# Layer 1 of a two-layer MoE behind banded and strided attention: token blocks of 512, 256 and four of 384 instead of six of 384

## The chip, the cores and the metric

The kernel runs on one core of a Trainium2 chip. The metric is the device time of one execution in microseconds. The engines are TensorE (PE; its weight loads are listed as PEld), VectorE (DVE), ScalarE (ACT), GpSimd (POOL) and SyncE (SP), which issues all DMAs here.

## The reference

Attention over 4 batches, 8 heads, 576 positions of 64 dimensions; the first four heads see the last 32 positions, the other four every 32nd position back. Its output, 2304 tokens of 512, goes through two dense layers of 2048 hidden units:

```python
scores = np.matmul(q, k.transpose(0, 1, 3, 2)) / np.sqrt(D)
mask_local = (rel >= 0) & (rel < 32)                       # heads 0 to 3
mask_strided = (rel >= 0) & (pos[None, :] % 32 == pos[:, None] % 32)   # heads 4 to 7
attn = softmax(np.where(mask, scores, -1e9)) ; x = (attn @ v) as (2304, 512)
h = np.maximum(x @ w_in, 0.0) ; x = (h * h) @ w_out        # layer 1
h = x @ w_in2 ; P = a0 + a1*h + a2*h*h + a3*h**3 ; Q = 1 + |b0|*|h| + |b1|*h*h
out = (P / (Q + 1e-6)) @ w_out2                            # layer 2
```

The weights arrive as 64-bit floats.

## The kernel before

The tokens are cut into six blocks of 384 (`TB`). A layer goes block by block; in a block the 16 hidden tiles `f` of 128 units are its steps. A step has a hidden unit (`h_unit`, L383: 12 matmuls of 128x128 by 384 columns, four slices `kk` of x times three products of high and low halves) and, two steps later (`LAG`), an output unit (`o_unit1`, L423: 12 more), which adds into four PSUM banks `acc`. Between them `act1` makes relu, square, a high part `gh` (ScalarE) and a low part `gl` (DVE in block 0, GpSimd later). At a block's end `evac1` stores the sums into a scratch in DRAM, from which layer 2 loads its x again (`load_x1`). Layer 2 works on 384-token blocks in the same way with a rational function (`act2`), its output units (L608) with 512 columns and six units behind.

Weights come as pairs of 32-bit words. `to_f32` (L161 on ScalarE, L162 to L164 on DVE) makes float32 of half a tile of weights and `split_w` (L180, L181 on GpSimd) its high and low parts. In block 0 `feed_w(2)` converts two halves each step, up to eight raw loads ahead; raw tiles lie in places of weight tiles not yet in use (`homes`). In blocks 1 to 4 the weights of layer 2 are converted in the same way and spilled to DRAM (`spills` counts halves by block).

Attention is cut into 14 pieces (`ORDER`): for each batch two strided ones (heads 4 and 5, 6 and 7), for each token block a local one (heads 0 to 3). Pieces 0 to 2 run first, ahead of all else, since block 0 needs them: strided, strided, local. The others are put between the steps of layer 1 by `PLAN`: at step (j, f) the scores and the softmax and the load of the next piece's queries and keys, two steps later the transposes of the exponentials, a step after that the values and x (`at_out`: a high copy on ScalarE, the low rest on DVE). x has three pairs of tiles in turn, each with all four slices: slices 0 and 1 are the local heads, 2 and 3 the strided ones.

A scheduler orders each engine's instructions when the kernel is built, by program order among what it takes to be ready, and places waits; instructions in `keep` stay in program order on their engine. SP's queue is in order too: a load that waits for its buffer holds those behind it.

The last five steps of layer 1's last block (`EARLY`) alternate with the first five units of layer 2, and among those `unit2` issues loads of layer 2's next block:

```python
if j + 1 < NB and f in (1, 4, 7, 10):
    load_x1(j + 1, f // 3)
```

Of the kernel before, what the change touches and what calls it, by code (L numbers as in the profile page):

```python
# [25 lines left out]
NB = NT // TB  # L26
# [38 lines left out]
def _local_window(J, j):  # L65

    first = (TB * J + STRIDE * j) % S == 0
    return STRIDE * j + (STRIDE if first else 0)


def _pack_qkv(q, k, v):

    tok = lambda x: x.transpose(1, 0, 2, 3).reshape(H, NT, D)
    qs = np.zeros((B * 2, P, QKS_W), np.float32)
    vs = np.zeros((B * 2, P, 2, 6, D), np.float32)
    a, c3 = np.arange(NA), np.arange(3)
# [13 lines left out]
    vl = np.zeros((NB, 2, P, 12, D), np.float32)  # L90
    qt, kt, vt = tok(q), tok(k), tok(v)
    for J in range(NB):
        for hp in range(2):
            for r in range(2):
                h, rows, t0 = 2 * hp + r, slice(r * D, (r + 1) * D), TB * J
                ql[J, hp, rows, :TB] = qt[h, t0 : t0 + TB].T
                lo = max(0, t0 - STRIDE)
                ql[J, hp, rows, TB + STRIDE - (t0 - lo) :] = kt[h, lo : t0 + TB].T
                for j in range(12):
                    w0 = t0 - STRIDE + _local_window(J, j)  # L100
                    vl[J, r, hp * D : (hp + 1) * D, j] = vt[h, w0 : w0 + 64]
    return qs, vs.reshape(B * 2, P, V_W), ql, vl.reshape(NB, 2, P, V_W)
# [8 lines left out]
def moe_kernel(ctx, tc, qs, vs, ql, vl, w1, w2, a, b, masks, eye, out):  # L111
    nc = tc.nc

    x1_dram = nc.dram_tensor("x1_scratch", (NB, P, KT * TB), F32, kind="Internal").ap()
# [5 lines left out]
    xpool = ctx.enter_context(tc.tile_pool(name="xpool", bufs=6))  # L120
# [9 lines left out]
    sms = [cpool.tile([P, 24], F32, name=f"sm{i}") for i in range(4)]  # L130
# [88 lines left out]
    def load_qk(p):  # L219
        if p.strided:  # L220
# [3 lines left out]
            return  # L224
        for hp in range(2):
            if p.n < HEAD:
                t = wpool.tile([P, QKL_W], F32, tag=("wh7", "wl7")[hp], name=f"qk{p.name}_{hp}")
            else:
                t = apool.tile([P, QKL_W], F32, tag="qk", name=f"qk{p.name}_{hp}")
            nc.sync.dma_start(t, ql[p.at, hp])  # L230
            p.qk.append(t)

    def load_v(p):
# [5 lines left out]
        for r in range(2):  # L239
            if p.n < HEAD:  # L240
                t = wpool.tile([P, 12, D], F32, tag=("wh6", "wl6")[r], name=f"v{p.name}_{r}")
            else:
                t = apool.tile([P, 12, D], F32, tag="v", name=f"v{p.name}_{r}")
            nc.sync.dma_start(t, vl[p.at, r].rearrange("p (j d) -> p j d", d=D))
            p.v.append(t)

    def at_scores(p):
# [5 lines left out]
        for r in range(2):  # L253
            flat = p.ps[r][:, : 6 * p.w]
# [28 lines left out]
        for m in range(3):  # L283
            for hp in range(2):
                for c in range(4):
                    j = 4 * m + c
                    k0 = QL_W + _local_window(p.at, j)
# [4 lines left out]
    def at_softmax(p, r):  # L292
        sm = sms[(2 * p.n + r) % len(sms)]
        to, mask = p.masks[r]
        s3 = p.ps[r][:, : 6 * p.w].rearrange("p (a k) -> p a k", k=p.w)
        if p.n >= MASK_PE:
            nc.vector.tensor_tensor(to, to, mask, ALU.add)
        nc.vector.tensor_reduce(sm[:, 0:6], s3, AX.X, ALU.max)  # L298
# [8 lines left out]
        wide = lambda c: sm[:, c : c + 6, None].to_broadcast([P, 6, p.w])  # L307
        nc.vector.tensor_tensor(ev, s3, wide(0), ALU.subtract)
        nc.scalar.activation(ev, ev, AF.Exp, scale=1.0 / 8.0)
        nc.vector.tensor_reduce(sm[:, 6:12], ev, AX.X, ALU.add)  # L310
        nc.vector.tensor_scalar(sm[:, 12:18], sm[:, 6:12], 1e-9, None, ALU.add)
        nc.vector.reciprocal(sm[:, 18:24], sm[:, 12:18])
        nc.gpsimd.tensor_tensor(ev, ev, wide(18), ALU.mult)
# [12 lines left out]
    def at_values(p):
# [15 lines left out]
        for j in range(12):  # L342
# [9 lines left out]
    def at_out(p):  # L352
        if not p.strided:
            x = x_block(p.at)
            for hp in range(2):
                split_x([z[:, hp, :] for z in x], p.o[hp][:, :TB])
            return
        a0 = 0
        while a0 < NA:
            t0 = p.at * S + a0 * STRIDE  # L360
            na = min(NA - a0, (TB - t0 % TB) // STRIDE)
            x = x_block(t0 // TB)
            for i, (base, nu) in enumerate(S_SLOTS):
                views = [
                    z[:, p.hp, t0 % TB : t0 % TB + na * STRIDE]
# [19 lines left out]
    def act1(j, f, ps):  # L385
        psum_h = j == NB - 1 and f >= NF - EARLY
        if psum_h:
            nc.scalar.activation(ps[:, :TB], ps[:, :TB], AF.Relu)
            nc.scalar.activation(ps[:, :TB], ps[:, :TB], AF.Square)
            h = ps[:, :TB]  # L390
        else:
            h = gpool.tile([P, TB], F32, tag="r", name=f"r{j}_{f}", bufs=4)
            nc.scalar.activation(h, ps[:, :TB], AF.Relu)  # L393
# [4 lines left out]
        gh = gpool.tile([P, TB], F32R, tag="gh", name=f"gh0_{j}_{f}", bufs=3)  # L398
        gl = gpool.tile([P, TB], F32R, tag="gl", name=f"gl0_{j}_{f}", bufs=3)
# [15 lines left out]
    def o_unit1(j, f):  # L415
# [4 lines left out]
        for e in range(KT):  # L420
            c = slice(DM + e * P, DM + (e + 1) * P)
            for i, (w, g) in enumerate(((wh, gh), (wh, gl), (wl, gh))):
                nc.tensor.matmul(acc[j][e][:, :TB], w[:, c], g, start=(f == 0 and i == 0), stop=(f == NF - 1 and i == 2))  # L423

    def evac1(j):
        for e, p in enumerate(acc.pop(j)):
            t = gpool.tile([P, TB], F32, tag="r", name=f"x1_{j}_{e}", bufs=4)
            if e % 2:
                nc.vector.tensor_copy(t, p[:, :TB])
            else:  # L430
                nc.scalar.copy(t, p[:, :TB])
            nc.sync.dma_start(x1_dram[j][:, e * TB : (e + 1) * TB], t)
# [3 lines left out]
    warm = gpool.tile([P, TB], F32, tag="r", name="warm", bufs=4).bitcast(BF16)[:, :512]  # L436
# [121 lines left out]
    def act2(j, f, ps):  # L558
# [74 lines left out]
    PLAN = {3: (0, 0), 4: (0, 5), 5: (0, 10), 6: (1, 1), 7: (1, 7), 8: (2, 0), 9: (2, 5), 10: (2, 10), 11: (3, 0), 12: (3, 5), 13: (3, 10)}  # L633
# [22 lines left out]
    spills = (0, 8, 16, 24, 2 * NF)  # L656
# [57 lines left out]
```

## Time and profile before

| | us |
|---|---|
| median of 3 runs | 893.65 (893.38 to 894.51) |
| the profiled execution | 892.89 |
| its span on the core | 891.1 |
| PE busy | 865.2 (97%) |
| DVE busy | 624.5 (70%) |
| GpSimd busy | 535.0 (60%) |
| ScalarE busy | 486.4 (55%) |

The span is the time between the first and the last instruction on the core. Busy times are unions of an engine's instructions. Matmuls overlap in the records, so their lengths say less than the distances between their starts.

### The profile page before, as it was taken

What the parts mean: (1) busy time and instruction counts of PE and PEld (TensorE: products, weight loads), DVE (VectorE), ACT (ScalarE), POOL (GpSimd) and SP (SyncE); (2) the same over time, 40 slices, a digit from 0 to 9 for tenths busy, and PEclk for the clock granted to TensorE, in tenths of its full rate; (3) what the DMA queues carried; (4) which work ended last, traced back from release to release, by engine and by line L of the source; (5) the groups of instructions that cost most, each with busy time, mean ns of one, the idle gap of its engine ahead of it and who ended that gap; (6) DMA issues with size and microseconds to landing.
All of it is one profiled execution on the core that took longest, in us unless ns stands there. A gap on an engine that the chain in (4) does not pass through costs nothing.

```text
span 891.1 us, 16392 instructions
## 1 busy us (share of the span) xinstructions
PE 865.2 (97%) x6312; PEld 807.2 (91%) x6312; DVE 624.5 (70%) x791; ACT 486.4 (55%) x1017; POOL 535.0 (60%) x555
## 2 busy tenths in 40 slices
PE   6798899999999999999999999999999999999998
PEld 4688789999999999999999999999999999999996
DVE  6798884655656765344115798888888888888885
ACT  4455533433433433333236777767767867867763
POOL 2477664444544544543234687877877877776773
PEclk8799999999999999999999999999999999999999
DMA  9881455645455443532684500100100100000000
GB/s 346 298 306 55 138 169 180 192 151 167 143 202 167 142 133 97 176 119 74 228 295 171 187 18 10 50 13 10 50 14 10 47 17 10 35 1 1 36 1 35
DMA packets 38957, 100.10 MB, mean 112 GB/s; under 512 B 4576, under 2 KB 10976, under 8 KB 38880
## 3 DMA queue, kind: packets, MB, share of 16 engines
q1 hardware_dynamic: 38880, 99.07, 32.5%
q8 instruction: 49, 0.80, 0.4%
q14 instruction: 28, 0.23, 0.1%
HBM read 72.84 MB, written 26.21 MB: 111 GB/s over the span
## 4 chain that ended last, share of the span: by engine, by line
PE 86%; DVE 5%; DMA 3%; ACT 2%; POOL 2%; issue 1%; SPq 0%; POOLq 0%; DVEq 0%; ACTq 0%
PE h L383 42%; PE acc L608 22%; PE acc L423 18%; PE ps_vl L330 1%; DMA qks<-in_qs 1%; DMA qkl<-in_ql 1%; PE ps_vs L330 1%; PE ps_tl L320 1%; DVE r L397 1%; POOL wl L181 1%; PE ps_sl L269 1%; DVE sm L298 1%; ACT w L161 1%; DVE w L164 1%; DVE sm L310 1%
## 5 line engine op out<-in xcount | busy, mean ns | idle before, releaser
L383 PE MATMUL h<-xh,wh 128*128 128x384 f32 x768 | 262.4, 342 | 1.0 <-POOL wh L180 0.4
L383 PE MATMUL h<-xh,wl 128*128 128x384 f32 x768 | 259.4, 338 | 1.3 <-POOL wl L181 1.2
L383 PE MATMUL h<-xl,wh 128*128 128x384 f32 x768 | 258.8, 337 | 0.0
L577 DVE RECIPROCAL h<-w 128x384 f32<-128x384 f32 x96 | 245.2, 2554 | 0.7 <-POOL w L574 0.7
L573 POOL TENSOR_TENSOR p<-p,hs 128x384 f32<-128x384 f32 x96 | 97.6, 1017 | 112.8 <-ACT p L571 112.8
L383 PEld LDWEIGHTS h<-xh,wh 128*128 128x128 f32 x768 | 145.3, 189 | 7.5 <-POOL wh L180 1.2
L383 PEld LDWEIGHTS h<-xl,wh 128*128 128x128 f32 x768 | 145.1, 189 | 4.1 <-DVE xl L350 0.2
L383 PEld LDWEIGHTS h<-xh,wl 128*128 128x128 f32 x768 | 145.1, 189 | 2.5 <-POOL wl L181 2.4
L401 POOL TENSOR_TENSOR gl<-r,gh 128x384 fp32r<-128x384 f32 x75 | 76.8, 1025 | 117.3 <-ACT gh L400 115.2
L423 PE MATMUL acc<-gh,wl 128*128 128x384 f32 x384 | 128.5, 336 | 2.3 <-POOL wl L181 2.3
L423 PE MATMUL acc<-gh,wh 128*128 128x384 f32 x384 | 128.8, 335 | 0.5 <-POOL wh L180 0.5
L423 PE MATMUL acc<-gl,wh 128*128 128x384 f32 x384 | 128.5, 335 | 0.0
L397 DVE TENSOR_TENSOR r<-r 128x384 f32<-128x384 f32 x75 | 54.7, 729 | 104.8 <-ACT r L393 101.3
L393 ACT ACTIVATE r<-h 128x384 f32<-128x384 f32 x91 | 44.6, 491 | 141.8 <-PE h L383 127.4
L608 PE MATMUL acc<-wh,gl 128*128 128x512 f32 x288 | 113.9, 395 | 0.0
L608 PE MATMUL acc<-wl,gh 128*128 128x512 f32 x288 | 113.7, 395 | 0.0
L608 PE MATMUL acc<-wh,gh 128*128 128x512 f32 x288 | 111.9, 389 | 0.0
L568 ACT ACTIVATE sq<-h 128x384 f32<-128x384 f32 x96 | 47.6, 496 | 110.2 <-PE h L383 106.6
L575 DVE SCALAR_TENSOR_TENSOR p<-p,co,h 128x384 f32<-128x384 f32 x96 | 58.6, 611 | 65.6 <-POOL p L573 65.6
L594 POOL TENSOR_TENSOR gl<-rq,gh 128x384 fp32r<-128x384 f32 x96 | 98.2, 1023 | 2.0 <-ACT gh L593 2.0
L574 POOL TENSOR_TENSOR w<-w,sq 128x384 f32<-128x384 f32 x96 | 97.7, 1018 | 0.0
L400 ACT CAST gh<-r 128x384 fp32r<-128x384 f32 x91 | 46.7, 513 | 62.3 <-DVE r L397 61.8
(105 smaller groups left out, 1373.2 us busy)
## 6 DMA issues: line engine op xcount, KB each, us to landing
wraw<-in_w SPq DMA_DIRECT2D x64, 512.0 KB, 4.4
w_scratch<-sph SPq DMA_DIRECT2D x32, 256.0 KB, 3.4
w_scratch<-spl SPq DMA_DIRECT2D x32, 256.0 KB, 3.1
wh<-w_scratch SPq DMA_DIRECT2D x16, 512.0 KB, 3.6
wl<-w_scratch SPq DMA_DIRECT2D x16, 512.0 KB, 4.5
qkl<-in_ql SPq DMA_DIRECT2D x12, 400.0 KB, 5.3
qks<-in_qs SPq DMA_DIRECT2D x8, 585.0 KB, 5.2
vl<-in_vl SPq DMA_DIRECT2D x12, 384.0 KB, 4.4
```

What stands on the lines that cost most here:

```text
L383: nc.tensor.matmul(ps[:, :TB], w[:, c], x[:, kk, :], start=(kk == 0 and i == 0), stop=(kk == KT - 1 and i == 2))
L397: nc.vector.tensor_tensor(h, h, h, ALU.mult)
L400: last_act = nc.scalar.copy(gh, h).ins
L401: low = lambda: (nc.vector if psum_h or j == 0 else nc.gpsimd).tensor_tensor(gl, h, gh.bitcast(F32), ALU.subtract)
L423: nc.tensor.matmul(acc[j][e][:, :TB], w[:, c], g, start=(f == 0 and i == 0), stop=(f == NF - 1 and i == 2))
L568: keep(nc.scalar.activation(sq, h, AF.Square))
L573: keep(nc.gpsimd.tensor_tensor(p1, p1, hs, ALU.mult))
L574: keep(nc.gpsimd.tensor_tensor(w, w, sq, ALU.add))
L575: keep(nc.vector.scalar_tensor_tensor(p1, p1, a1, h, ALU.add, ALU.mult))
L577: keep(nc.vector.reciprocal(h, w))
L594: keep(nc.gpsimd.tensor_tensor(gl, rq, gh.bitcast(F32), ALU.subtract))
L608: nc.tensor.matmul(p, g[:, t * P : (t + 1) * P], w[:, c], start=(f == 0 and i == 0), stop=(f == NF - 1 and i == 2))
```

## The change

The blocks of layer 1 get widths 512, 256, 384, 384, 384, 384; layer 2 keeps 384. All that goes by layer 1's blocks takes its width from the list: local pieces (piece 2 of block 0 now has 512 tokens, piece 3 of block 1 256), their loads, masks and softmax, x, hidden and output units, the scratch. x is held in tiles by head kind: the local half (slices 0, 1) in two buffers in turn, the strided half (2, 3) in three, for both layers. The transposed exponentials are written over the exponentials and no longer into tiles of their own. `PLAN` moves the pieces: 3 from (0, 0) to (0, 2), 4 from (0, 5) to (0, 6), 5 stays at (0, 10), 6 from (1, 1) to (1, 2), 7 from (1, 7) to (2, 1), and so on.

```diff
+WIDTHS = (512, 256, 384, 384, 384, 384)
+NB = len(WIDTHS)
+STARTS = tuple(sum(WIDTHS[:j]) for j in range(NB + 1))
...
-    x1_dram = nc.dram_tensor("x1_scratch", (NB, P, KT * TB), F32, kind="Internal").ap()
+    x1_dram = nc.dram_tensor("x1_scratch", (P, KT, NT), F32, kind="Internal").ap()
...
-    xpool = ctx.enter_context(tc.tile_pool(name="xpool", bufs=6))
+    xpool = ctx.enter_context(tc.tile_pool(name="xpool", bufs=1))
...
-    def x_block(j):
-        if j not in xt:
-            xt[j] = tuple(xpool.tile([P, KT, TB], F32R, tag="x", name=f"x{c}0_{j}") for c in "hl")
-        return xt[j]
+    def x_half(layer, j, half):
+
+        n = j % (2, 3)[half]
+        if (layer, j, half) not in xt:
+            xt[layer, j, half] = tuple(
+                xpool.tile([P, 2, 384 if n else 512], F32R, tag=f"x{c}{half}{n}", name=f"x{c}{half}{layer}_{j}") for c in "hl")
+        return xt[layer, j, half]
+
+    def x_rows(layer, j, kk, w):
+        return [z[:, kk % 2, :w] for z in xt[layer, j, kk // 2]]
...
+            self.cb = 3 if self.strided else WIDTHS[at] // P
+            self.nb = 2 * self.cb
...
         if p.homes:
-            both = wpool.tile([P, 2, 6, EW], F32, tag="w" + p.homes[r], name=f"ea{p.name}_{r}")
-            e, p.t[r] = both[:, 0], both[:, 1]
+            e = wpool.tile([P, n, EW], F32, tag="w" + p.homes[r], name=f"ea{p.name}_{r}")
         else:
-            e = apool.tile([P, 6, EW], F32, tag="e", name=f"e{p.name}_{r}", bufs=3)
+            e = apool.tile([P, 6, EW], F32, tag="e", name=f"e{p.name}_{r}", bufs=3)[:, :n]
...
-        for m in range(3):
+        for m in range(p.cb):
             src = p.e[r][:, 2 * m : 2 * m + 2, :].rearrange("p a k -> p (a k)")
             pin(p, nc.tensor.transpose(ps[:, m * P : (m + 1) * P], src, ident))
-        if r not in p.t:
-            p.t[r] = apool.tile([P, 6, EW], F32, tag="at", name=f"at{p.name}_{r}")
-        p.t[r] = p.t[r].rearrange("p a k -> p (a k)")
-        nc.scalar.copy(p.t[r], ps[:, : 3 * P])
+        p.t[r] = p.e[r].rearrange("p a k -> p (a k)")
+        nc.scalar.copy(p.t[r], ps[:, : p.cb * P])
...
     def h_unit(layer, j, f, ps):
-        xh, xl = xt[j]
+        n = TB if layer else WIDTHS[j]
         wh, wl = wt[layer, f]
         for kk in range(KT):
             c = slice(kk * P, (kk + 1) * P)
+            xh, xl = x_rows(layer, j, kk, n)
             for i, (w, x) in enumerate(((wh, xh), (wh, xl), (wl, xh))):
-                nc.tensor.matmul(ps[:, :TB], w[:, c], x[:, kk, :], start=(kk == 0 and i == 0), stop=(kk == KT - 1 and i == 2))
+                nc.tensor.matmul(ps[:, :n], w[:, c], x, start=(kk == 0 and i == 0), stop=(kk == KT - 1 and i == 2))
...
     def load_x1(j, kk):
-        if kk == 0:
-            xt[j] = tuple(xpool.tile([P, KT, TB], F32R, tag="x", name=f"x{c}1_{j}") for c in "hl")
-        xh, xl = xt[j]
+        x_half(1, j, kk // 2)
+        xh, xl = x_rows(1, j, kk, TB)
...
-    PLAN = {3: (0, 0), 4: (0, 5), 5: (0, 10), 6: (1, 1), 7: (1, 7), 8: (2, 0), 9: (2, 5), 10: (2, 10), 11: (3, 0), 12: (3, 5), 13: (3, 10)}
+    PLAN = {3: (0, 2), 4: (0, 6), 5: (0, 10), 6: (1, 2), 7: (2, 1), 8: (2, 6), 9: (2, 11), 10: (3, 1), 11: (3, 6), 12: (3, 11), 13: (4, 2)}
...
-    spills = (0, 8, 16, 24, 2 * NF)
+    spills = (0, 5, 14, 23, 2 * NF)
```

## Rows read from the trace of the kernel before

**Rows 1.** The first page, part 1: busy time of each engine.
```profile
PE 865.2 (97%) x6312; PEld 807.2 (91%) x6312; DVE 624.5 (70%) x791; ACT 486.4 (55%) x1017; POOL 535.0 (60%) x555
```

**Rows 2.** Timeline of PE, 12 to 41 us: start, length, instruction [idle before].
```profile
13.44 1.58 PE L269 MATMUL ps_sl<-qkl 64*32 64x64 f32 x96
...
22.54 2.78 PE L330 MATMUL ps_vl<-eal,vl 64*64 64x32 f32 x94 [0.22 <-ACT eal L324]
...
25.96 0.66 PE L383 MATMUL h<-xh,wh 128*128 128x384 f32 x1
...
39.16 1.69 PE L320 MATMUL ps_tl<-ident,el 128*128 128x128 f32 x6 [6.07 <-POOL el L313]
```

**Rows 3.** Windows: stretch, length; busy by engine; clock, DMA share, GB/s.
```profile
20.00:30.00 10.00, 9.78 (x132) 8.05 (x126) 6.70 (x15) 2.99 (x10) 5.81 (x8) 0.57 0.97 383
...
25.90:131.40 105.50, 92.65 (x915) 84.86 (x915) 90.46 (x161) 53.36 (x110) 69.36 (x75) 0.94 0.53 184
131.40:887.40 756.00, 754.36 (x4990) 709.98 (x4988) 518.33 (x585) 421.73 (x882) 457.39 (x464) 1.00 0.28 94
...
400.00:500.00 100.00, 100.00 (x579) 100.00 (x578) 35.93 (x44) 41.71 (x87) 37.29 (x38) 1.00 0.56 201
```

**Rows 4.** One line each: L383, L423, then L264, L269, L320, L330.
```profile
25.90:131.40 105.50, 48.12 (x228) 42.09 (x228) 0.94 0.53 184
...
25.90:131.40 105.50, 37.94 (x192) 33.75 (x193) 0.94 0.53 184
...
25.90:131.40 105.50, 1.07 (x5) 0.23 (x4) 0.94 0.53 184
...
25.90:131.40 105.50, 4.39 (x288) 3.65 (x288) 0.94 0.53 184
...
25.90:131.40 105.50, 3.76 (x18) 2.40 (x18) 0.94 0.53 184
...
25.90:131.40 105.50, 3.63 (x184) 3.14 (x184) 0.94 0.53 184
```

**Rows 5.** The chain in order of time: start, length, what.
```profile
492.08 4.16 PE acc L423 x24
...
873.01 14.34 PE acc L608 x63
```

**Rows 6.** Timeline of ScalarE, 35 to 39 us.
```profile
36.67 2.30 ACT L161 ACTIVATE w<-wraw 128x512 f32<-128x512 f32 x4
```

**Rows 7.** Timeline of weight loads, 56.8 to 57 us.
```profile
56.81 0.19 PEld L383 LDWEIGHTS h<-xh,wh 128*128 128x128 f32 x1
56.92 0.19 PEld L383 LDWEIGHTS h<-xl,wh 128*128 128x128 f32 x1
```

**Rows 8.** Groups by form: line, engine, shapes, count, busy us, mean ns.
```profile
L298 DVE TENSOR_REDUCE sm<-ps_sl 128x6 f32<-128x384 f32 x12 | 6.1, 549 | 0.4 <-PE ps_sl L269 0.4
...
L313 POOL TENSOR_TENSOR eal<-eal,sm 128x384 f32<-128x384 f32 x2 | 1.6, 831 | 3.8 <-ACT w L161 3.8
```

**Rows 9.** Timeline of PE, 123 to 136 us, piece 6.
```profile
124.03 1.17 PE L269 MATMUL ps_sl<-qkl 64*32 64x64 f32 x96
...
133.89 0.55 PE L320 MATMUL ps_tl<-ident,el 128*128 128x128 f32 x3 [0.16 <-POOL el L313]
```

**Rows 10.** Timelines of ScalarE, PE and DVE, 475 to 500 us.
```profile
475.78 0.53 ACT L553 CAST xh<-xraw 128x384 fp32r<-128x384 f32 x1
...
485.88 0.49 ACT L568 ACTIVATE sq<-h 128x384 f32<-128x384 f32 x1 [1.54 <-PE h L383]
...
488.79 0.49 ACT L388 ACTIVATE h<-h 128x384 f32<-128x384 f32 x1
...
487.59 0.33 PE L383 MATMUL h<-xh,wl 128*128 128x384 f32 x1
...
494.00 0.33 PE L423 MATMUL acc<-gh,wh 128*128 128x384 f32 x1
...
492.55 0.54 DVE L401 TENSOR_TENSOR gl<-h,gh 128x384 fp32r<-128x384 f32 x1
```

More of the change, by code (lines that the diff above doesn't have):

```diff
@@ L65, in _local_window, with _key_start @@
 def _local_window(J, j):
-    first = (TB * J + STRIDE * j) % S == 0
-    return STRIDE * j + (STRIDE if first else 0)
+    first = (STARTS[J] + STRIDE * j) % S == 0
+    return STRIDE * (j if first else j - 1)
+def _key_start(J):
+    return max(0, STARTS[J] - STRIDE)
 def _pack_qkv(q, k, v):
@@ L89, in _pack_qkv @@
     ql = np.zeros((NB, 2, P, QKL_W), np.float32)
-    vl = np.zeros((NB, 2, P, 12, D), np.float32)
+    vl = np.zeros((NB, 2, P, 16, D), np.float32)
     qt, kt, vt = tok(q), tok(k), tok(v)
-    for J in range(NB):
+    for J, w in enumerate(WIDTHS):
         for hp in range(2):
             for r in range(2):
[L95 to L100, printed above, removed]
+                h, rows, t0 = 2 * hp + r, slice(r * D, (r + 1) * D), STARTS[J]
+                ql[J, hp, rows, :w] = qt[h, t0 : t0 + w].T
+                lo = _key_start(J)
+                ql[J, hp, rows, w : 2 * w + t0 - lo] = kt[h, lo : t0 + w].T
+                for j in range(w // STRIDE):
+                    w0 = t0 + _local_window(J, j)
                     vl[J, r, hp * D : (hp + 1) * D, j] = vt[h, w0 : w0 + 64]
-    return qs, vs.reshape(B * 2, P, V_W), ql, vl.reshape(NB, 2, P, V_W)
+    return qs, vs.reshape(B * 2, P, V_W), ql, vl.reshape(NB, 2, P, VL_W)
 def _pack_w(w_in, w_out):
@@ L129, in moe_kernel @@
     co = cpool.tile([P, 16], F32, name="co")
-    sms = [cpool.tile([P, 24], F32, name=f"sm{i}") for i in range(4)]
+    sms = [cpool.tile([P, 32], F32, name=f"sm{i}") for i in range(4)]
     wt = {}
@@ L306, in at_softmax @@
         ev = e[:, :, : p.w]
-        wide = lambda c: sm[:, c : c + 6, None].to_broadcast([P, 6, p.w])
+        wide = lambda c: sm[:, c : c + n, None].to_broadcast([P, n, p.w])
         nc.vector.tensor_tensor(ev, s3, wide(0), ALU.subtract)
         nc.scalar.activation(ev, ev, AF.Exp, scale=1.0 / 8.0)
[L310 to L313, printed above, removed]
+        nc.vector.tensor_reduce(sm[:, 8 : 8 + n], ev, AX.X, ALU.add)
+        nc.vector.tensor_scalar(sm[:, 16 : 16 + n], sm[:, 8 : 8 + n], 1e-9, None, ALU.add)
+        nc.vector.reciprocal(sm[:, 24 : 24 + n], sm[:, 16 : 16 + n])
+        nc.gpsimd.tensor_tensor(ev, ev, wide(24), ALU.mult)
         p.e[r] = e
@@ L317, in at_transpose @@
         ps = psum.tile([P, 512], F32, tag="ps", name=f"ps_t{p.name}_{r}")
-        for m in range(3):
+        for m in range(p.cb):
             src = p.e[r][:, 2 * m : 2 * m + 2, :].rearrange("p a k -> p (a k)")
             pin(p, nc.tensor.transpose(ps[:, m * P : (m + 1) * P], src, ident))
-        if r not in p.t:
-            p.t[r] = apool.tile([P, 6, EW], F32, tag="at", name=f"at{p.name}_{r}")
-        p.t[r] = p.t[r].rearrange("p a k -> p (a k)")
-        nc.scalar.copy(p.t[r], ps[:, : 3 * P])
+        p.t[r] = p.e[r].rearrange("p a k -> p (a k)")
+        nc.scalar.copy(p.t[r], ps[:, : p.cb * P])
     def at_values(p):
@@ L341, in at_values @@
             return
-        for j in range(12):
+        for j in range(4 * p.cb):
             for i in range(2):
@@ L353, in at_out @@
         if not p.strided:
-            x = x_block(p.at)
+            w = WIDTHS[p.at]
+            x_half(0, p.at, 0)
             for hp in range(2):
-                split_x([z[:, hp, :] for z in x], p.o[hp][:, :TB])
+                split_x(x_rows(0, p.at, hp, w), p.o[hp][:, :w])
             return
@@ L360, in at_out @@
             t0 = p.at * S + a0 * STRIDE
-            na = min(NA - a0, (TB - t0 % TB) // STRIDE)
-            x = x_block(t0 // TB)
+            J = max(j for j in range(NB) if STARTS[j] <= t0)
+            na, at = min(NA - a0, (STARTS[J + 1] - t0) // STRIDE), t0 - STARTS[J]
+            x = x_half(0, J, 1)
             for i, (base, nu) in enumerate(S_SLOTS):
                 views = [
-                    z[:, p.hp, t0 % TB : t0 % TB + na * STRIDE]
+                    z[:, p.hp % 2, at : at + na * STRIDE]
                     .rearrange("p (a r) -> p a r", r=STRIDE)[:, :, base : base + 3 * nu]
@@ L422, in o_unit1 @@
             for i, (w, g) in enumerate(((wh, gh), (wh, gl), (wl, gh))):
-                nc.tensor.matmul(acc[j][e][:, :TB], w[:, c], g, start=(f == 0 and i == 0), stop=(f == NF - 1 and i == 2))
+                nc.tensor.matmul(acc[j][e][:, : WIDTHS[j]], w[:, c], g, start=(f == 0 and i == 0), stop=(f == NF - 1 and i == 2))
     def evac1(j):
+        w = WIDTHS[j]
         for e, p in enumerate(acc.pop(j)):
-            t = gpool.tile([P, TB], F32, tag="r", name=f"x1_{j}_{e}", bufs=4)
+            t = g_tile("r", f"x1_{j}_{e}", w)
             if e % 2:
-                nc.vector.tensor_copy(t, p[:, :TB])
+                nc.vector.tensor_copy(t, p[:, :w])
             else:
-                nc.scalar.copy(t, p[:, :TB])
-            nc.sync.dma_start(x1_dram[j][:, e * TB : (e + 1) * TB], t)
+                nc.scalar.copy(t, p[:, :w])
+            nc.sync.dma_start(x1_dram[:, e, STARTS[j] : STARTS[j] + w], t)
     nc.vector.memset(co[:, 8:9], 1.0 + 1e-6)
-    warm = gpool.tile([P, TB], F32, tag="r", name="warm", bufs=4).bitcast(BF16)[:, :512]
+    warm = g_tile("r", "warm", 256).bitcast(BF16)
     nc.vector.memset(warm, 1.0)
@@ L547, in load_x1 @@
     def load_x1(j, kk):
-        if kk == 0:
-            xt[j] = tuple(xpool.tile([P, KT, TB], F32R, tag="x", name=f"x{c}1_{j}") for c in "hl")
-        xh, xl = xt[j]
+        x_half(1, j, kk // 2)
+        xh, xl = x_rows(1, j, kk, TB)
         raw = l2.tile([P, TB], F32, tag="xraw", name=f"xraw{j}_{kk}", bufs=3)
-        nc.sync.dma_start(raw, x1_dram[j][:, kk * TB : (kk + 1) * TB])
-        keep(nc.scalar.copy(xh[:, kk], raw))
-        keep(nc.gpsimd.tensor_tensor(xl[:, kk], raw, xh[:, kk].bitcast(F32), ALU.subtract))
+        nc.sync.dma_start(raw, x1_dram[:, kk, j * TB : (j + 1) * TB])
+        keep(nc.scalar.copy(xh, raw))
+        keep(nc.gpsimd.tensor_tensor(xl, raw, xh.bitcast(F32), ALU.subtract))
     open2, due = [], []
```

56 lines of the change are left out of this document (31 added, 25 removed).

## The prediction

> **What bounds the kernel now.** I read the page first, then the windows, the chain, and the timelines of the places that the diff touches. PE is busy 97% of the span [rows 1], and the chain runs on its matmuls, so only work taken off PE, or time in which PE waits or runs slowly, is worth anything. The change takes no matmul off PE: the columns are the same, only cut differently. So the question is where PE loses time, and the windows say: early. From the first hidden matmul (25.96 us, [rows 2]) to the start of block 1's output matmuls (131.4) the stretch is 105.5 us long [rows 3]. In it PE ran 228 + 192 = 420 layer matmuls and 1.07 + 4.39 + 3.76 + 3.63 = 12.85 us of attention [rows 4]. A layer matmul of 384 columns costs 4.16/24 = 173.3 ns back to back [rows 5], so 420 cost 72.8 us. 105.5 - 72.8 - 12.85 leaves **19.9 us lost**: 105.5 - 92.65 = 12.9 us show as idle, the other 7 are half-speed clock (mean 0.94 of full) and short gaps at each switch between attention and layer. The stretch 400 to 500 us shows PE busy all the time at full clock [rows 3]. The gain must come out of the 19.9.
>
> The largest single loss is a hole of 6.07 us before piece 3's transposes at 39.16 [rows 2]. Piece 3 stands at step (0, 0), so its softmax lies in ScalarE's order ahead of the weight conversions; the next four conversions start only behind its exponentials, at 36.67 [rows 6]. The other losses are waits for converted weights: a step of block 0 needs two half tiles, and DVE is busy 90.46 of the 105.5 us [rows 3], PE only 92.65 of it.
>
> **Wider block 0, narrower block 1.** A 384-column matmul costs 173.3 ns, one of 512 costs 14.34 us/63 = 227.6 ns [rows 5] (the last one's drain included, so slightly less). The line through both is 54.3 ns for 128 columns, so 256 would cost 119 ns, and 512 + 256 costs what two times 384 costs: 227.6 + 119 = 346.6 against 346.7 ns. No change from the sum of widths; I carry +-1.7 us (4.4 ns on 384 matmuls, the accuracy of the line). Bounds for 256, which no row shows: below, 108 ns, since two full weight loads start 0.11 us apart [rows 7]; above, 173.3, if the loads set the pitch. I take 119, since the pitch follows the columns from 384 to 512.
>
> What it buys: a step of block 0 lasts 24 x 227.6 = 5.5 us of PE instead of 4.16, over the same two conversions. DVE's work in the stretch (90.46 us, of which a little belongs to block 1) grows by about 16 x 0.18 = 3 us for wider low parts, while PE's block 0 becomes 88 us plus some 11 of attention. PE is then the longer one by a few microseconds, and the conversions start about 8 us earlier because piece 3 no longer stands ahead of them. So the weights are ahead of PE instead of behind it.
>
> **Piece 3 later, at (0, 2).** With it move its masks and scores on PE, the softmax on DVE, ScalarE and GpSimd, and on SP the load of piece 4's queries and keys. On SP that load waits for piece 3's scores, which free its buffer, and holds up the weight loads behind it; two steps' raw loads (four) now go ahead of it. The transposes come two steps after, 4 x 12 x 227.6 ns = 10.9 us, against 8.7 us from scores to exponentials at piece 6 (below). The hole goes: -6.1 and about -1 of the slow clock behind it. Where the stall goes next: to PE's start, and to o of unit 0, whose weights are then ready.
>
> **What stays lost in the stretch.** Unit 0 still starts on a slow clock (0.57 in 20 to 30 us [rows 3]): 2.0. Short gaps at the switches: 1.2. Waits for pieces 3 to 5: 1.8, by hand. Sum 5.0 (3 to 9). So **-14.9**.
>
> **Piece 2 is a third wider, and PE's first unit waits for it.** Scores 1.58 us +0.53; six DVE steps of 0.55 +1.1; two GpSimd multiplications of 0.83 +0.55; values 2.78 for 94, so +1.0 for 128 [rows 2, 8]. Exponential, copies, one more transpose each: +0.3. Piece 3's masks no longer stand ahead: -0.3. Sum **+3.2** (1.6 if half hides behind other work, 5 if GpSimd puts a weight split of 2 us ahead). The loads ahead of the weights grow by 0.5 MB, at 383 GB/s [rows 3] 1.3 us; the first weights are converted well before PE starts, so nothing, and the 5 covers it. Piece 3 is a third narrower: -1.4 on PE (a third of 1.69 us transposes, and as much again for scores and for values), but its masks (0.5) now fall behind the start: **-0.9**.
>
> **Piece 6 at (1, 2).** Between its scores and its transposes lie two steps as before, but steps of block 1 are now 24 x 119 = 2.86 us: 5.7 us. Today scores start at 124.03 and the transposes at 133.89, with 0.16 us of waiting for the exponentials [rows 9]: the softmax took 133.89 - 125.2 = 8.7. So PE waits up to 3, and behind such a wait the clock can fall, as behind the hole: 0 to 4. Program order is not forced there and other units can be drawn ahead: **+1.5**.
>
> **Two buffers for the local half of x instead of three.** Layer 2's block 1 takes the buffer of layer 1's block 5. Its first copy on ScalarE stands today at 475.78, long before the last hidden unit of block 5 has read its x (487.59) [rows 10]. It is pinned in order, so the activations of layer 2's units 2 and 3 wait behind it to about 487.1. They then take 2.9 us each (485.88 to 488.79), and the relu of block 5's last unit, today at 488.79, comes behind both: 487.5 + 5.8 = 493.3, 4.5 later. Its low part is ready at 493.09 and wanted at 494.00, slack 0.9. So PE waits 3.6, or 0.7 if the relu gets between them, or 0 if the order lets it ahead; DVE's order can add one: 0 to 4.5, taken **+3**. Behind it the second layer runs 8 us late against its matmuls, which lag six units of 4.2 us behind; that covers it.
>
> At nothing: the transposed exponentials written over the exponentials (the copy waits for the transposes anyway; the ring of three is held one step longer, and pieces are at least four steps apart), x split by head kind (same copies), the scratch's layout (the same stores), spills spread 5, 9, 9, 9 (same count, by width), pieces 7 to 13 a few steps later (each ahead of the block that needs it; PE loses 756.00 - 754.36 = 1.6 us in all that comes after [rows 3], and 384-wide steps stay).
>
> **Sum:** -14.9 + 3.2 - 0.9 + 1.5 + 3 = **-8.1 us**. The profiled execution took 892.89 us (span 891.1, 1.8 around it), so it would be 884.8; the median of the runs, 893.65, is 0.8 higher: **885.5**. Its own range: 880.5 to 891.
>
> **Rivals.**
> *Weight loads set the pitch at 256 columns.* 384 matmuls at 173.3 instead of 119 ns: +20.8, so +12.7 in all, 906. It decides from 119 + 8.1/0.384 = 140 ns on. For it: weight loads are busy 100.00 of 100.00 us in 400 to 500 [rows 3], and none is seen back to back faster than the matmuls. Against it: the pair 0.11 us apart [rows 7]. Chance 0.05. The Trainium skill (Perfetto Trace Analysis, Identifying the Most-Contended Engine) bids one judge TensorE's headroom by the share in which weight loads are busy, not by matmuls. By that rule layer 1 has no headroom in its loads, a narrower matmul would gain nothing, and the sum would be this rival's 906; by the pair of loads it is 885.5. The row speaks against the rule here, since a load's shown length (0.19) is longer than the distance at which the next can start.
>
> *The weights still bind block 0.* DVE's order, not its sum, keeps PE waiting as now, and only hole and clock (7) go: -7 + 3.2 - 0.9 + 1.5 + 3 = -0.2, 893.5. For it: DVE's 93 us against PE's 99 is close. Chance 0.12.
>
> *The hole stays.* PE's order again puts piece 3's transposes behind its scores with no unit between; 7 of the gain is gone: -1.1, 892.5. Chance 0.07.
>
> *Both narrow places cost full price and a slow clock after:* 4 + 1 at piece 6, 4.5 + 1 at the layers' border: +6 on the sum, -2.1, 891.5. Chance 0.11.
>
> *Nothing new waits:* lost 3, start +1.6, neither narrow place: -16.2, 877.5. Chance 0.05.
>
> **The numbers.** My forecast has 0.60. Runs of this kernel differ by 1.1 us in 893.65, so 0.2% (1.8 us) is about what can be told from no change. Faster by more: 0.58 of the forecast's 0.60, the last rival's 0.05, half of "both narrow places" (0.06), 0.04 of the weights and 0.03 of the hole: 0.76. Within: the rest of these, 0.11. Slower: 0.05 of the loads and 0.08 for the far ends of the weights and the narrow places: 0.13. The range goes from "nothing new waits" to just above the before, where all bounds of the forecast meet (lost 9, start 5, 4, 4.5: +1.7): 877 to 895.
>
> **What would show it.** Right: the first hidden matmul near 29 us; no gap over 2 us before piece 3's transposes; PE busy nearly all of 35 to 130 us; 120 ns between matmuls of block 1; a late copy and a gap of some 3 us where block 5's last outputs run; the same second layer, some 8 us earlier. Wrong: gaps in block 0 ended by GpSimd's weight splits, a pitch over 140 ns in block 1, or piece 2 ending after 31 us.

## The result, and the profile after

The new kernel takes **884.15 us** (median of 4 runs, 882.28 to 885.44) against 893.51 for the kernel before on the same chip: a ratio of 0.9899, 95% interval 0.9886 to 0.9913, so 8 to 10 us faster. The forecast was 885.5, between 877 and 895. The profiled execution took 884.73 us, its span is 883.0.

The first part of the page of the kernel after, to be held against [rows 1]:

```profile
PE 862.4 (98%) x6312; PEld 792.1 (90%) x6312; DVE 616.1 (70%) x791; ACT 489.4 (55%) x1017; POOL 531.0 (60%) x555
```

PE's instructions are as many as before and its busy time is 2.8 us less; the rest of the gain is time in which PE had waited. The windows of the kernel after, cut where [rows 3] were cut (first hidden matmul, block 1's first output matmul, last matmul), and one of 10 us that matters below:

```profile
30.80:135.60 104.80, 103.71 (x850) 84.49 (x850) 89.31 (x157) 55.69 (x106) 71.10 (x75) 0.98 0.50 165
135.60:879.20 743.60, 737.96 (x4990) 693.12 (x4989) 508.97 (x588) 420.32 (x882) 450.51 (x463) 1.00 0.29 95
...
140.00:150.00 10.00, 8.30 (x138) 7.75 (x137) 5.20 (x11) 3.58 (x8) 5.50 (x7) 0.83 0.42 138
```

The first stretch is as long as before (104.8 against 105.5 us), but it now holds the hidden and output units of a wider block. The same stretch of the kernel after by PE's lines, as in [rows 4]: L401 and L446 (hidden and output matmuls), then L281, L286, L337 and L345 (masks, scores, transposes, values).

```profile
30.80:135.60 104.80, 53.47 (x228) 0.98 0.50 165
...
30.80:135.60 104.80, 46.20 (x192) 0.98 0.50 165
...
30.80:135.60 104.80, 1.55 (x6) 0.98 0.50 165
...
30.80:135.60 104.80, 3.87 (x256) 0.98 0.50 165
...
30.80:135.60 104.80, 2.24 (x16) 0.98 0.50 165
...
30.80:135.60 104.80, 2.95 (x152) 0.98 0.50 165
```

What a matmul costs is read from the chain (12 matmuls of 512 columns a row) and from the timeline of PE in block 1 (starts of two matmuls of 256 columns), both of the kernel after:

```profile
44.60 2.72 PE h L401 x12
47.32 2.73 PE acc L446 x12
```

```profile
137.10 0.28 PE L401 MATMUL h<-xh,wh 128*128 128x256 f32 x1
137.22 0.28 PE L401 MATMUL h<-xl,wh 128*128 128x256 f32 x1
```

2.72/12 = 226.7 ns for 512 columns and 120 ns between starts at 256. The stretch holds 384 of the first and 36 of the second: 87.0 + 4.3 = 91.4 us, and 10.6 of attention. 104.8 - 91.4 - 10.6 = **2.8 us lost, where 19.9 were lost before**. That is the gain. Attention costs 2.2 us less there (12.85 before).

The timeline of PE at the two places where the forecast expected a change, piece 2's values with the first hidden matmul, and piece 3's transposes (before: [rows 2]):

```profile
26.10 3.63 PE L345 MATMUL ps_vl<-eal,vl 64*64 64x32 f32 x126 [0.38 <-ACT eal L339]
30.80 1.01 PE L401 MATMUL h<-xh,wh 128*128 128x512 f32 x2 [1.07 <-ACT xh L364]
...
49.89 0.60 PE L337 MATMUL ps_tl<-ident,el 128*128 128x128 f32 x4
```

The hole of 6.07 us is gone: no idle time is printed before the transposes. PE starts on hidden units 4.84 us later than before (25.96). What is lost behind the stretch is read from PE's timeline at piece 6 (scores, then transposes; before: [rows 9]) and at the border of the layers, with ScalarE's copy and the relu behind it there (before: [rows 10]):

```profile
133.02 1.17 PE L286 MATMUL ps_sl<-qkl 64*32 64x64 f32 x96
...
141.60 0.55 PE L337 MATMUL ps_tl<-ident,el 128*128 128x128 f32 x3 [1.46 <-POOL el L330]
...
481.56 0.45 PE L401 MATMUL h<-xh,wh 128*128 128x384 f32 x1 [0.71 <-DVE rq L609]
```

```profile
477.76 0.51 ACT L576 CAST xh<-xraw 128x384 fp32r<-128x384 f32 x1 [0.55 <-PE h L401]
478.80 0.47 ACT L411 ACTIVATE h<-h 128x384 f32<-128x384 f32 x1 [0.53 <-PE h L401]
```

PE waits 1.46 us for piece 6's exponentials and the granted clock falls behind that wait (0.83 in 140 to 150 us). At the border the copy stands late, but the relu comes directly behind it. PE's wait of 0.71 us is not at block 5's last outputs: it stands before a hidden matmul of the second layer and ends with VectorE's `rq`, the result of the rational function. The list of PE's waits in the kernel after names the places together (us in total, times, longest):

```profile
PE ps_tl L337 <- POOL el L330: 4.6, 7, 1.5
...
PE h L401 <- DVE rq L609: 0.7, 1, 0.7
```

**The sum as measured.** Start +4.8; lost in the stretch 2.8 - 19.9 = -17.1; attention in it -2.2. Behind it the stretch is 12.4 us shorter (743.6 against 756.0), while 91.4 - 72.8 = 18.6 us of matmuls have moved ahead of it, so 6.2 us are lost there: 4.0 as more idle time (5.64 against 1.64), the rest a slow clock behind the waits and short gaps. Together -8.3 us; the spans differ by 8.1.

### The profile page after: what moved, and what is told of

It reads as the page before. It is cut to its first block, busy times and chain, and to the rows that moved or that the text cites. A ratio compares the mean times of both kernels' runs of the same rounds, so it can differ in the third digit from the quotient of the medians.

```text
span 883.0 us, 16434 instructions
## 1 busy us (share of the span) xinstructions
PE 862.4 (98%) x6312; PEld 792.1 (90%) x6312; DVE 616.1 (70%) x791; ACT 489.4 (55%) x1017; POOL 531.0 (60%) x555
## 4 chain that ended last, share of the span: by engine, by line
PE 87%; DVE 6%; DMA 2%; ACT 2%; POOL 1%; issue 1%; SPq 0%; ACTq 0%; DVEq 0%; POOLq 0%
PE h L401 42%; PE acc L631 23%; PE acc L446 18%; PE ps_vl L345 1%; PE ps_ss L286 1%; DMA co<-in_b 1%; ACT w L168 1%; DMA x_scratch<-x 1%; DVE sm L316 1%; DVE bits L170 1%; DVE sm L328 1%; DVE r L420 0%; PE ps_vs L345 0%; DVE sm L327 0%; DVE wraw L171 0%
## 5 line engine op out<-in xcount | busy, mean ns | idle before, releaser
L401 PE MATMUL h<-xh,wh 128*128 128x384 f32 (+2 forms) x768 | 262.3, 342 | 3.2 <-ACT r L416 1.4
L401 PE MATMUL h<-xh,wl 128*128 128x384 f32 (+2 forms) x768 | 258.9, 337 | 0.0
L401 PE MATMUL h<-xl,wh 128*128 128x384 f32 (+2 forms) x768 | 258.6, 337 | 0.0
L401 PEld LDWEIGHTS h<-xh,wh 128*128 128x128 f32 x768 | 145.2, 189 | 11.7 <-ACT r L416 1.9
L401 PEld LDWEIGHTS h<-xl,wh 128*128 128x128 f32 x768 | 145.2, 189 | 6.3
L401 PEld LDWEIGHTS h<-xh,wl 128*128 128x128 f32 x768 | 145.1, 189 | 2.6
L424 POOL TENSOR_TENSOR gl<-r,gh 128x384 fp32r<-128x384 f32 (+1 forms) x75 | 71.7, 956 | 111.7 <-ACT gh L423 104.3
L446 PE MATMUL acc<-gh,wl 128*128 128x384 f32 (+2 forms) x384 | 128.9, 336 | 0.0
L446 PE MATMUL acc<-gl,wh 128*128 128x384 f32 (+2 forms) x384 | 128.9, 336 | 0.0
L446 PE MATMUL acc<-gh,wh 128*128 128x384 f32 (+2 forms) x384 | 128.4, 336 | 0.0
L420 DVE TENSOR_TENSOR r<-r 128x384 f32<-128x384 f32 (+1 forms) x75 | 49.0, 654 | 106.6 <-ACT r L416 99.2
L416 ACT ACTIVATE r<-h 128x384 f32<-128x384 f32 (+2 forms) x91 | 44.6, 490 | 126.1 <-PE h L401 114.9
L423 ACT CAST gh<-r 128x384 fp32r<-128x384 f32 (+2 forms) x91 | 46.7, 514 | 56.0 <-DVE r L420 55.4
```

The source lines that it names most:

```text
L401: nc.tensor.matmul(ps[:, :n], w[:, c], x, start=(kk == 0 and i == 0), stop=(kk == KT - 1 and i == 2))
L420: nc.vector.tensor_tensor(h, h, h, ALU.mult)
L423: last_act = nc.scalar.copy(gh, h).ins
L424: low = lambda: (nc.vector if psum_h or j == 0 else nc.gpsimd).tensor_tensor(gl, h, gh.bitcast(F32), ALU.subtract)
L446: nc.tensor.matmul(acc[j][e][:, : WIDTHS[j]], w[:, c], g, start=(f == 0 and i == 0), stop=(f == NF - 1 and i == 2))
```

## The experiments

Each kernel was timed beside the kernel before on its chip (893.0 to 893.5 us), and has one profile, of one of its executions.

**1. Even blocks with the rest of the change.** The widths go back to six times 384, with an offset of the masks and the spills to match; the plan, the x tiles and the exponentials in place stay.

```diff
-WIDTHS = (512, 256, 384, 384, 384, 384)
+WIDTHS = (384, 384, 384, 384, 384, 384)
...
-                c0 = C_L + (0, 4, 1, 0, 3, 1)[p.at] * EW
+                c0 = C_L + (0, 3, 1, 0, 3, 1)[p.at] * EW
...
-    spills = (0, 5, 14, 23, 2 * NF)
+    spills = (0, 8, 16, 24, 2 * NF)
```

> The changed kernel with six even blocks of 384 again, all else of the change kept (plan, x tiles, exponentials in place; the spills 8 a block as before). Theory A (two gains: the later piece 3 closes the hole, the wide block covers the weight conversions): the hole is gone, the first hidden matmul comes at about 25.5 us, but PE waits for converted weights in block 0 again; about 886 to 888. Theory B (the width does it all, moving piece 3 is worth nothing): 893, as before. Theory C (the plan does it all, the width only costs the later start): 879 to 880, faster than the change.

Measured 892.47 us, ratio 0.9994 (0.9984 to 1.0003): the time of theory B. One row of PE's timeline and two of its list of waits in this kernel, then the same two of the list in the kernel before:

```profile
47.84 0.55 PE L337 MATMUL ps_tl<-ident,el 128*128 128x128 f32 x3 [3.18 <-POOL el L330]
```

```profile
PE acc L446 <- POOL wl L188: 3.6, 6, 1.3
...
PE h L401 <- POOL wl L188: 1.5, 3, 0.7
```

```profile
PE acc L423 <- POOL wl L181: 2.3, 4, 0.8
...
PE h L383 <- POOL wl L181: 1.2, 2, 0.7
```

With piece 3 later in even blocks its hole shrinks to 3.18 us, but PE's waits for converted weights, high and low parts together, grow from 4.4 to 6.1 us in the stretch, and its first 6 us run at a mean granted clock of 0.51, against 0.79 before. Part of the stall moved on, and little was won.

**2. The wide block with piece 3 at its old place.**

```diff
-    PLAN = {3: (0, 2), 4: (0, 6), ...
+    PLAN = {3: (0, 0), 4: (0, 6), ...
```

> The changed kernel with piece 3 back at step (0, 0), all else kept. Theory A: the hole of about 6 us before piece 3's transposes is back, with a slow clock behind it, and the conversions of the weights start behind its exponentials; about 889 to 891. Theory B (in a wide block two units cover the softmax and nothing is lost): 884.

Measured 889.82 us (five runs, 888.78 to 894.38), ratio 0.9977 (0.9955 to 1.0): theory A. That it is faster than the kernel before is not clear of the noise. PE's timeline of this kernel shows a smaller hole, in two parts, at the old place:

```profile
42.94 0.55 PE L337 MATMUL ps_tl<-ident,el 128*128 128x128 f32 x2 [1.98 <-POOL el L330]
44.39 0.69 PE L337 MATMUL ps_tl<-ident,el 128*128 128x128 f32 x2 [0.90 <-POOL el L330]
```

Held side by side, each against the kernel before on its chip: all but the widths 0.6 us less, all but the later piece 3 3.2 us less, everything 9.4 us less. The gain is not the sum of the two. The stretch from the first hidden matmul to block 1's first output matmul shows why; its windows in experiment 1, then in experiment 2:

```profile
25.77:130.32 104.55, 94.08 (x916) 85.40 (x917) 90.52 (x156) 50.69 (x106) 70.88 (x75) 0.95 0.54 184
```

```profile
31.74:145.44 113.70, 108.14 (x849) 87.06 (x849) 91.17 (x157) 55.77 (x107) 69.88 (x74) 0.95 0.49 161
```

Less the layer matmuls (72.8 and 91.4 us, as above) and the attention in them (12.5 and 11.5 us), 19.2 and 10.8 us are lost, against 19.9 in the kernel before and 2.8 in the kernel after. So the later piece 3 is worth 0.7 us in even blocks and 8.0 in the wide one. The wide block alone is worth 9.1 there, but it pays for most of that with a later start (31.74 us) and with the waits behind the stretch.

**3. More steps between scores and transposes of the local pieces 6, 7, 10 and 13.**

```diff
-        for step, do in ((0, sc), (2, tr_both), (3, va)):
+        gap = 2 if pieces[n].strided or n < 6 else 4 if n == 6 else 3
+        for step, do in ((0, sc), (gap, tr_both), (gap + 1, va)):
```

> The changed kernel with more steps between scores and transposes of the local pieces from 6 on: four for piece 6, three for pieces 7, 10 and 13. The waits of PE for these exponentials (4.6 us by the list of waits) and some 1.8 us of slow clock behind piece 6 are taken for lost time. If they are: 877.5 to 879.5. Rival: PE waits there because DVE and GpSimd are late in all they do at a block's beginning, so it waits elsewhere: 883 to 885.

Measured **877.67 us**, ratio 0.9829 (0.9814 to 0.9843), 6.5 us below the kernel after. The windows from 136 to 200 us, first of this kernel, then of the kernel after:

```profile
136.00:200.00 64.00, 64.00 (x685) 63.47 (x671) 35.11 (x67) 24.18 (x56) 29.79 (x34) 1.00 0.54 173
```

```profile
136.00:200.00 64.00, 60.94 (x639) 59.30 (x639) 32.00 (x61) 23.78 (x56) 28.34 (x33) 0.97 0.52 158
```

PE is never idle there now, the clock stays full, and 46 more of PE's instructions run in the same time. So the theory holds. Experiments 4 and 5 below differ by the same edit, and by 5.8 us.

**4. The second layer's block 1 loaded later.**

```diff
-        if j + 1 < NB and f in (1, 4, 7, 10):
-            load_x1(j + 1, f // 3)
+        at = (6, 8, 10, 12) if j == 0 else (1, 4, 7, 10)
+        if j + 1 < NB and f in at:
+            load_x1(j + 1, at.index(f))
```

> The changed kernel, but the four loads of layer 2's block 1 stand at its units 6, 8, 10 and 12 instead of 1, 4, 7 and 10, behind the last reader of the local x buffer. Theory A (the shared buffer costs the 0.7 us that PE idles at 481.56): 883 to 883.7. Theory B (it costs 3 us, the rest hidden in a second layer that runs later): 881. Theory C (nothing, PE makes it up): 884.

Measured 882.65 us, ratio 0.9881 (0.9864 to 0.9897): 1.5 below the kernel after, with intervals that overlap. Two windows of 470 to 490 us, of this kernel and of the kernel after:

```profile
470.00:490.00 20.00, 20.00 (x117) 20.00 (x116) 13.30 (x15) 12.53 (x26) 8.87 (x9) 1.00 0.59 218
```

```profile
470.00:490.00 20.00, 19.29 (x111) 18.97 (x110) 10.71 (x13) 13.43 (x28) 9.24 (x10) 1.00 0.59 210
```

The wait of 0.71 us is gone. So the copies do cost at the border, but less than a microsecond of idle time. The rest of the 1.5 us need not be theirs: in this execution the clock did not fall behind piece 6's wait (told below), and with experiment 3's edit in both kernels the later copies are worth 0.8 us (experiment 5 against 3).

**5. Both repairs (3 and 4).**

> The kernel after with both earlier repairs: the longer distance from scores to transposes for pieces 6, 7, 10 and 13, and the second layer's block 1 loads at units 6, 8, 10 and 12. Theory: the two cost different places (block 1's wait for piece 6, the border of the layers), so their gains add: 877.7 - 1.5 = 876.2 us (875.5 to 877). Rival: with the first repair the last outputs of block 5 no longer wait, or the second one's 1.5 us was only the later units' good luck: 877.7 as with the first alone. In the trace no gap over 0.5 us with transposes as the waiting matmuls behind 31 us, and none before a hidden matmul of the second layer.

Measured 876.86 us (875.66 to 877.96), ratio 0.982 (0.9805 to 0.9834): inside the range of the theory (875.5 to 877), but about half way from its 876.2 to the rival's 877.7, and 0.8 us below the third experiment, which the intervals don't tell apart.

**6. Both repairs and 8 dummy matmuls instead of 6 ahead of the masks.**

```diff
-    warm_up(6)
+    warm_up(8)
```

> As the one with both repairs, and the first run of matmuls on the dummy tile is 8 long instead of 6, so that it reaches to the arrival of the masks (PE idle 0.67 us there today). In the kernel after the masks, scores and dummy matmuls from 4.89 to 10.06 us run at half the pace that they had in the kernel before (masks 0.72 against 0.44 us, scores 1.54 against 0.92), although the row of granted clock says 1.00. Theory: TensorE had not yet come up to full pace in the wide kernel because of the idle stretch in front of the masks; with it filled the two pieces end near 8 us and the first hidden matmul comes 1 to 2 us earlier: 874 to 875.5. Rival: the later end of the two pieces lies beside the softmax of the first on VectorE and GpSimd and costs nothing, or the pace does not follow the filling: 876.2, the same as without.

Measured 876.25 us (875.48 to 877.01), ratio 0.9811 (0.9798 to 0.9825). The fastest kernel of the study, though not measurably faster than the fifth. The time is the rival's. In the profile the scores do run in 0.92 us and the first hidden matmul comes at 29.74 us, against 31.40 in experiment 5, and the two profiled executions differ by as much (876.30 and 877.96 us); but the profiled execution of experiment 5 is the slowest of its four, and the medians differ by 0.6 us only.

**7 and 8. One of VectorE's three steps of a conversion, which puts in the sign, left out in layer 1,** in even blocks (on top of 1) and in the kernel after.

```diff
-        nc.vector.scalar_tensor_tensor(bits, hi, -0x80000000, bits, ALU.bitwise_and, ALU.bitwise_or)
+        if layer:
+            nc.vector.scalar_tensor_tensor(bits, hi, -0x80000000, bits, ALU.bitwise_and, ALU.bitwise_or)
```

> Six blocks of 384 with the new order, and in layer 1 one of VectorE's three steps of a weight conversion is left out (the sign is not put in, so the weights are positive): some 30 steps of 0.69 us = 20.7 us less on VectorE in block 0. Theory: in even blocks the conversions' sum sets PE's pace (PE 88.7 of 99.2 us busy, VectorE 87.6), so most of the 10.5 us of idle PE and part of the slow clock go: 882 to 886. Rival: it is the order of the softmax and of the splits on GpSimd that keeps PE waiting, not VectorE's sum: 889 to 892.5.

> The kernel after with the same step of the conversion left out in layer 1. Theory: with block 0 of 512 PE is the longer one (93.1 of 94.2 us busy from 30.8 to 125 us), so a cheaper conversion buys only the gap of 1.1 us and up to 1 us at the start: 882 to 884.5. Rival: the wide block is still tied to the conversions in ways that do not show as idle time (short gaps at each switch, the slow clock): 876 to 880, the same gain as in even blocks.

Even blocks: 883.86 us, ratio 0.9897 (0.9883 to 0.9911), 8.6 us less than experiment 1. Wide block: 880.75 us, ratio 0.9863 (0.9848 to 0.9879), 3.4 us less than the kernel after; the first is where the theory has it, the second lies between theory and rival. The window of the stretch in the wide block, and the last low part of layer 1's weights there:

```profile
29.90:133.20 103.30, 103.27 (x851) 84.41 (x851) 71.00 (x125) 55.69 (x105) 69.69 (x73) 0.99 0.53 174
```

```profile
114.83 1.30 POOL L189 TENSOR_TENSOR wl<-w,wh 128x512 fp32r<-128x512 f32 x1
```

VectorE is busy 18 to 20 us less in the stretch of either kernel. In even blocks the stretch gets 9.4 us shorter (95.1 instead of 104.6). In the wide block the weights are ready 7.1 us sooner (121.96 in the kernel after), and the stretch gets only 1.5 us shorter. So VectorE's work on the conversions did bind the even blocks, and binds the wide one much less. Whether in even blocks it is the sum of that work or the longer time of each conversion, these runs don't separate. Part of the 3.4 was not in the theory: piece 6's transposes, in this kernel's timeline of PE, wait 0.18 us instead of 1.46; they come 6.1 us after the scores' end instead of 7.4, and why the softmax is shorter there was not followed further.

```profile
137.85 0.55 PE L338 MATMUL ps_tl<-ident,el 128*128 128x128 f32 x3 [0.18 <-POOL el L331]
```

**9 and 10. The kernel after with 8 and with 4 dummy matmuls.** The edit is that of experiment 6, and the same with 4.

> The kernel after with 8 instead of 6 dummy matmuls ahead of the masks. Theory: the pace of TensorE's first 10 us is not the change's: it depends on the idle stretch in front of the masks and differs between executions (0.63 to 0.77 us idle in the profiles so far, masks at 0.72 us in some and 0.45 in others); with the stretch filled the masks run in 0.45 to 0.55 us, scores in 0.92, the first hidden matmul comes near 29.5 instead of 30.8, and the time is 882.5 to 883.7. Rival: the wide kernel's start has its own cause, scores stay at 1.54 us, 884.2.

> The kernel after with 4 instead of 6 dummy matmuls ahead of the masks, so that PE idles about 1.5 us in front of them. Theory: always at half pace to about 10 us, masks 0.72 us and both scores 1.54, first hidden matmul at 30.8 to 31.2, 884.2 to 885.2. Rival: no difference from 6 or 8 dummy matmuls, 884.2 in all three.

Measured 882.45 us (ratio 0.9875, 0.986 to 0.989) and 882.87 (0.9883, 0.9866 to 0.9899). With 8 the time is about the theory's (882.5 to 883.7), but what was to bring it didn't come: the first masks and scores stay slow. With 4 it is 1.3 us below the least that the theory allowed. Neither is clearly below the kernel after, whose interval theirs overlap. Two rows of the timeline of PE with 8, then two with 4, each the first masks and scores:

```profile
5.03 0.72 PE L281 MATMUL ps_ss<-cst 128*128 128x324 bf16 x2
5.68 1.34 PE L286 MATMUL ps_ss<-qks 64*64 64x54 f32 x48
```

```profile
4.84 0.72 PE L281 MATMUL ps_ss<-cst 128*128 128x324 bf16 x2 [1.47 <-DMA cst<-in_masks]
5.49 1.54 PE L286 MATMUL ps_ss<-qks 64*64 64x54 f32 x48
```

The filled stretch didn't bring full pace from the start, the longer idle stretch didn't cost time, and the first hidden matmul came at 30.35 and 30.05 us.

## Why the prediction was right, and where its steps were not

The net, -8.1 us, is what the spans show, and the mechanism held: PE works through block 0 nearly without waiting (1.1 us idle in the stretch, 12.9 before), and behind the first hidden matmul it waits for no weights, where it waited 4.4 us. But its terms missed by 1.3 to 2.6 us, three to either side, and the misses cancelled to 0.2. That the sum is so near is luck; its sign and the way it came about are not.

- **"Lost in the stretch", -14.9:** measured -17.1. What was left is 2.8 us instead of 5.0: the waits for pieces 3 to 5, taken at 1.8, did not come (the transposes of piece 3 stand 10.95 us behind its scores, 10.9 in the forecast), and the one wait, of 1.1 us, is for ScalarE's relu. A step of its argument held only at first: "the conversions start about 8 us earlier because piece 3 no longer stands ahead of them". ScalarE's fourth conversion, the one behind the hole at 36.67 us before [rows 6], starts at 25.94 us in the kernel after. But the lead is soon used up: the sixth stands at 37.50, against 37.82, and the last low part of layer 1's weights is made only 1.3 us sooner. The row of ScalarE's fourth conversion in the kernel after, then the last such rows of GpSimd's timeline in the kernel before and after:

```profile
25.94 0.67 ACT L168 ACTIVATE w<-wraw 128x512 f32<-128x512 f32 x1
```

```profile
123.27 1.47 POOL L181 TENSOR_TENSOR wl<-w,wh 128x512 fp32r<-128x512 f32 x1
```

```profile
121.96 1.29 POOL L188 TENSOR_TENSOR wl<-w,wh 128x512 fp32r<-128x512 f32 x1
```

  Over the whole block the weights are hardly sooner; PE has more work per weight, and starts 4.8 us later. By the time the conversions end, PE has put 512 columns through each weight instead of 384, and that work is missing from the blocks behind. The hole and the weights were no separate gains of 7 and 8 either: in even blocks the later piece 3 won only 0.7 us (experiment 1), in the wide block 8.0, where with piece 3 early the hole was still 2.9 us and the last low part 10 us later, at 131.74 (experiment 2). The rival "the weights still bind block 0" was false for 512 columns and describes the even blocks, where VectorE's work on them is what binds (experiment 7).
- **Columns:** 226.7 and 120 ns, against 227.6 and 119 forecast. Weight loads do not hold the pitch at 173.3 ns when the columns are 256, so that rival is refuted. The Trainium skill (Perfetto Trace Analysis, Identifying the Most-Contended Engine) has TensorE's headroom judged by the share of peak FLOP/s and the share in which weight loads are busy. By the second, this case would have come out otherwise: in the trace of the kernel before that share was 100% in 400 to 500 us [rows 3], and the narrower matmuls nevertheless run at 120 ns.
- **Piece 2 wider, start +3.2:** measured +4.84 in this execution. The other wide kernels start between 29.7 and 31.7 us, so +3.8 to +5.8; the term was too small, inside its bounds (1.6 to 5) or over them by up to 0.8. In experiments 3 to 5 the wait before that matmul (1.4 to 1.9 us) ends with GpSimd's low part of a weight, the case that the forecast had priced at 5. Part of the scatter goes with TensorE's pace in the first 10 us, told below: the earliest, 29.74 and 29.93 us, are experiments 6 and 8, whose scores ran in 0.92 us.
- **Piece 3 narrower, -0.9:** attention costs 2.2 us less in the stretch; the 1.3 more are mostly the transposes, 2.24/16 = 140 ns each instead of 3.76/18 = 209 [rows 4]; piece 3's six behind the hole had taken 1.69 us [rows 2], where the clock was low (0.77 and 0.89 in 30 to 40 and 40 to 50 us). The forecast's own parts, three times a third of 1.69, make 1.7 rather than 1.4.
- **Piece 6, +1.5:** mis-sized: 1.46 us of idle time and, behind it, two groups of 12 matmuls that take 2.3 and 2.2 us from start to start instead of 1.44, so about 3.1, inside its bounds (0 to 4). From scores to transposes 141.6 - 134.2 = 7.4 us passed, against the 8.7 taken. The slow clock stands in this execution alone: in those of experiments 4, 9 and 10, whose code is the same there, PE waits 0.89, 0.96 and 0.94 us, and the granted clock stays at 1.00. The rows of experiment 9:

```profile
140.00:150.00 10.00, 8.80 (x154) 8.39 (x155) 4.85 (x8) 4.37 (x10) 5.48 (x7) 1.00 0.55 156
```

```profile
140.96 0.55 PE L337 MATMUL ps_tl<-ident,el 128*128 128x128 f32 x3 [0.96 <-POOL el L330]
```

- **Pieces 7 and 13** were put at nothing ("384-wide steps stay") and wait 1.4 and 1.2 us (piece 10: 0.3). That step failed: the softmax takes longer at the new places, and piece 7's two steps still hold an output unit of block 1 with 256 columns, so that PE comes 7.9 us after the scores instead of 8.4. Piece 13's scores and GpSimd's two multiplications that end its softmax, in the kernel before and in the kernel after:

```profile
319.82 1.17 PE L269 MATMUL ps_sl<-qkl 64*32 64x64 f32 x96
```

```profile
326.46 2.15 POOL L313 TENSOR_TENSOR el<-el,sm 128x384 f32<-128x384 f32 x2 [0.33 <-DVE sm L312]
```

```profile
341.66 1.17 PE L286 MATMUL ps_sl<-qkl 64*32 64x64 f32 x96
```

```profile
351.75 1.92 POOL L330 TENSOR_TENSOR el<-el,sm 128x384 f32<-128x384 f32 x2 [0.33 <-DVE sm L329]
```

  From the end of the scores to the end of the softmax that is 7.6 us before and 10.8 after; for piece 7 it is 8.5 and 9.7. Why it is slower there was not followed. Experiment 3 shows what the waits of pieces 6, 7, 10 and 13 are worth together: 6.5 us against the kernel after, 5.8 between experiments 4 and 5.
- **The layers' border, +3:** 0.71 us. That this is the middle one of the three figures named (0.7) is chance. The order was another: the relu came directly behind the late copy and ahead of most of the activations that the forecast had put before it, block 5's outputs did not wait, and the wait fell on a hidden matmul of the second layer. Experiment 4 shows that the copies' place causes it.

## What to carry to other kernels

When one engine prepares an operand that the matmuls consume, and its total time is near theirs, moving the preparation's neighbours mostly moves the stall (0.7 of 19.9 us won here). Giving the matmuls more columns per prepared operand in that stretch wins more (9.1), and the two together nearly all (17.1). A distance counted in steps is a time that changes with the width of a step: after a change of widths, look at every place where one engine's result is wanted a fixed number of steps later, and at places that only moved too, since the result itself can take longer there (pieces 7 and 13). Piece 6's wait cost twice its idle time in the one execution in which the clock was slow behind it; three others show the wait without the slow clock.

## What was not expected of the hardware

In the first 10 us the same matmuls ran at two paces while the row of granted clock says 1.00 throughout: 48 scores in 0.92 us in the kernel before and in experiments 1, 6 and 8, in 1.54 or 1.55 us in the kernel after and in experiments 2 to 5, 7 and 10, and in 1.34 us in experiment 9 (the first 48 of each kernel). It goes neither with the widths (7 is even, 6 and 8 are wide) nor simply with the idle stretch ahead of the masks (filled in 6 and 9, and only 6 was fast from the start). Its cause stays open; with one profile of each kernel it isn't shown whether the pace belongs to the kernel or changes from execution to execution. Both pieces' scores are over by 10.3 us even at the slow pace (by 8.0 in the kernel before), and the medians of experiments 9 and 10 differ by 0.4 us, less than runs of one kernel do.
